# Filler matmuls in the setup, and PE transposes cut into thirds, in an attention and gated-MLP kernel

## The chip, the cores and the metric

The kernel runs on one core of one Trainium2 chip. A core has a matrix engine (TensorE, PE in the profile, with its weight loads as PEld), a vector engine (VectorE, DVE), an activation engine (ScalarE, ACT), GpSimd (POOL) and a queue engine (SyncE, SP), which here issues most transfers. All of them run beside each other and are held together by semaphores. The metric is the device time of one execution in microseconds; lower is better.

## What is computed

Block-sparse attention is followed by a gated MLP with a spatial projection, for 4 batches, 8 heads, 768 positions, head size 64:

```python
scores = scale * np.matmul(q, k.transpose(0, 1, 3, 2))
scores = np.where(mask, scores, -1000000000.0)       # window, global and sampled 32x32 blocks
attn = np.exp(scores - max);  attn = attn / attn.sum(-1)
x = np.matmul(attn, v)                               # heads joined: (4, 768, 512)
h = np.maximum(x @ w_in, 0.0)                        # 1024 wide
u, v = h[..., :512], h[..., 512:]
v_n = (v - mean(v)) / np.sqrt(var(v) + 1e-06)
v_s = np.einsum('ts,bsd->btd', w_spatial, v_n) + b_spatial[None, :, None]
out = (u * v_s) @ w_out
```

## The kernel before

Heads are taken in 16 pairs (p = 0 to 15, four pairs to a batch). A pair is 12 **slots** (s = 0 to 11), two heads of six key chunks. The main loop, lines 414 to 470, is an order written out by hand: it is the order in which every engine gets its instructions, and each engine works through its own in that order.

One slot does the following. `qk_exp` (L239) makes the scores of one chunk of 128 keys against all 768 queries, two PE matmuls of 384 columns into one of two PSUM buffers, and one ACT exponential (L248) that reads that buffer. The block mask is no separate step: 24 extra rows of `kt` (block indicator, `ind`) and `qt` (mask values, made once by the matmuls at L208) add a large negative number where a block is not allowed. `av` (L253) multiplies finished exponentials of seven slots ago with v, six PE matmuls of 65 columns; after each sixth, `norm` (L267) divides on DVE. A unit of the MLP of the batch before follows when there is one: `moe_units` (L313) makes them in four kinds (L332, L355, L377, L395), and they start in slot 9 of pair 4. In slot 8, `xtr` (L277) transposes the normalised output of the pair before, for three pairs of a batch by a DMA transpose on SP's queue and for the fourth by six PE transposes (L283) with a DVE copy behind them.

q and k come in as float32 and go through several hands. `load` (L91) puts three transfers of a pair on SP's queue, three pairs ahead, into two staging buffers per tensor. `prepare` (L116) casts them to bf16 on POOL, in slot 7, two pairs ahead. Then they have to be transposed. Pair 0 is done head by head on PE (`tr_head`, L188). Pairs 1 to 4 are done by `tr_pair` (L195): six PE transposes of 128x128 and two DVE copies, k and q each in one slot (slots 7 and 10 for pair 1, slots 5 and 9 after that). From pair 5 on, `tr_dma` (L225) issues DMA transposes on SP's queue in slot 10 two pairs ahead, and `split_pair` (L230) copies the halves to their places on DVE, k in slot 5 and q in slot 9. SP issues everything in program order, and an instruction that waits holds up those behind it; the same is true of DVE, where `split_pair(5, "k")` (slot 5 of pair 4) stands ahead of the last normalisation of pair 3 (slot 6).

The spatial weights (`ws_nat`) come in on POOL's queue, are transposed on PE in six units of six transposes (`wspt_unit`, L292) in slots 3, 7 and 11 of pairs 2 and 3, and are copied by DVE into `w_spt`. `w_in` and `w_out` follow on POOL's queue.

The setup (L122 to L221) starts the loads, runs eight PE matmuls on zeros into a scratch bank (L143 to L145), makes the mask's parts on POOL and DVE (`ind` is copied by POOL at L160 and moved into `kt` by DVE at L180), and transposes the first head.

Of the kernel before, what the change touches and what calls it, by code (L numbers as in the profile page):

```python
# [10 lines left out]
FP32 = mybir.dt.float32  # L11
BF16 = mybir.dt.bfloat16
I32 = mybir.dt.int32
AF = mybir.ActivationFunctionType
# [12 lines left out]
def kernel(  # L27
# [16 lines left out]
    nc = tc.nc  # L44

    B, H, S, D = q.shape
# [3 lines left out]
    NCH = S // 128  # L50
# [6 lines left out]
    NG = H // 2  # L57
    NP = B * NG
    MASK_NEG = -300.0
    VA = D + 1  # L60
    KR = D + NB
# [3 lines left out]
    psum = ctx.enter_context(tc.tile_pool(name="psum", bufs=1, space=bass.MemoryType.PSUM))  # L65
    ctx.enter_context(tc.manual_schedule())

    ident = const.tile([128, 128], BF16)
    warm = const.tile([128, 512], BF16)
    w_in_t = const.tile([128, NDM, DFF], BF16)  # L70
    w_out_t = const.tile([128, NDH, DM], BF16)
    ws_nat = const.tile([128, NCH, S], BF16)
# [4 lines left out]
    qt = [const.tile([KR, S], BF16, name=f"qt{s}") for s in range(4)]  # L77
    kt = [const.tile([KR, S], BF16, name=f"kt{s}") for s in range(4)]
# [18 lines left out]
    nat = {}  # L97
# [5 lines left out]
    def cast_qk(p, nm, hs, eng):  # L103
        src = st[nm, p][:, hs].rearrange("p h (c d) -> p h c d", d=D)
        dst = nat[nm, p].rearrange("p c h d -> p h c d")[:, hs]
        if eng is nc.scalar:
            nc.scalar.activation(out=dst, in_=src, func=AF.Copy)
        else:
            eng.tensor_copy(out=dst, in_=src)  # L109

    def cast_v(p):
        nc.gpsimd.tensor_copy(  # L112
            out=vv[p % 3][:, :, :, 0:D],
            in_=st.pop(("v", p)).rearrange("p h (c d) -> p h c d", d=D))
# [18 lines left out]
    ind_nat = const.tile([NB, S], BF16)  # L133
    ind = const.tile([NB, S], BF16)
# [5 lines left out]
    nc.vector.memset(tiny, 0.0)  # L140
    nc.scalar.activation(out=tiny, in_=tiny, func=AF.Exp)

    wps = psum.tile([128, 512], FP32, tag="moe", bufs=2)  # L143
    for _ in range(8):
        nc.tensor.matmul(out=wps, lhsT=warm[:, 0:128], rhs=warm, start=True, stop=True)  # L145


    colidx = const.tile([NB, NB], FP32)
# [8 lines left out]
    nc.gpsimd.affine_select(out=ind_nat, in_=ind_nat, compare_op=ALU.not_equal, fill=1.0,  # L157
                            base=0, pattern=[[-1, NB], [0, BLK]], channel_multiplier=1)
    make_identity(nc, ident)
    nc.gpsimd.tensor_copy(out=ind, in_=ind_nat.rearrange("b (p c) -> b c p", c=NCH))  # L160

    for s in range(3):
        nc.gpsimd.memset(vv[s][:, :, :, D:VA], 1.0)
# [13 lines left out]
                            op0=ALU.subtract, op1=ALU.mult)  # L177
    cast_qk(0, "q", slice(0, 1), nc.vector)
    cast_qk(0, "k", slice(0, 1), nc.scalar)
    nc.vector.tensor_copy(out=kt[0][D:KR, :], in_=ind)  # L180

    def dve_copy(o, i):
        nc.vector.tensor_copy(out=o, in_=i)

# [3 lines left out]
    def tr_head(h, nm, copy):  # L188
        ps = psum.tile([128, S], BF16, tag="moe", bufs=2)
        for c in range(NCH):  # L190
            nc.tensor.transpose(out=ps[0:D, c * 128:(c + 1) * 128], in_=nat[nm, 0][:, c, h],
                                identity=ident)
        copy((qt if nm == "q" else kt)[h][0:D, :], ps[0:D, :])

    def tr_pair(p, nm):  # L195
        src = nat.pop((nm, p))
        ps = psum.tile([128, S], BF16, tag="moe", bufs=2)
        for c in range(NCH):
            nc.tensor.transpose(out=ps[:, c * 128:(c + 1) * 128],
                                in_=src[:, c].rearrange("p h d -> p (h d)"), identity=ident)  # L200
        for h in range(2):
            nc.vector.tensor_copy(out=(qt if nm == "q" else kt)[(2 * p + h) % 4][0:D, :],
                                  in_=ps[h * D:(h + 1) * D, :])

    tr_head(0, "k", dve_copy)
    mq = psum.tile([128, 1024], FP32, tag="sc", bufs=2, name="mq")
    for hf in range(2):
        nc.tensor.matmul(out=mq[0:NB, hf * 512:hf * 512 + HALF], lhsT=bm,  # L208
                         rhs=ind[:, hf * HALF:(hf + 1) * HALF], start=True, stop=True)
    act_copy(qt[0][D:KR, :].rearrange("p (b c) -> p b c", b=2),  # L210
             mq[0:NB].rearrange("p (b c) -> p b c", b=2)[:, :, 0:HALF])
    tr_head(0, "q", dve_copy)

    def mask_rows(sl):
        nc.vector.tensor_copy(out=kt[sl][D:KR, :], in_=kt[0][D:KR, :])
        nc.vector.tensor_copy(out=qt[sl][D:KR, :], in_=qt[0][D:KR, :])

    def second_head():
        mask_rows(1)
        cast_qk(0, "k", slice(1, 2), nc.vector)  # L220
        cast_qk(0, "q", slice(1, 2), nc.vector)  # L221
# [3 lines left out]
    def tr_dma(p, nm):  # L225
        tt[nm, p] = work.tile([128, NCH, 128], BF16, tag=f"tt_{nm}", bufs=2, name=f"tt_{nm}")
        nc.sync.dma_start_transpose(out=tt[nm, p],
                                    in_=nat.pop((nm, p)).rearrange("p c h d -> p (c h d)"))

    def split_pair(p, nm):  # L230
        src = tt.pop((nm, p)).rearrange("x c n -> x (c n)")
        for h in range(2):
            nc.vector.tensor_copy(out=(qt if nm == "q" else kt)[(2 * p + h) % 4][0:D, :],
                                  in_=src[h * D:(h + 1) * D, :])
# [4 lines left out]
    def qk_exp(j, ci):  # L239
        if ci == 0:  # L240
            a_ref[j] = work.tile([128, NCH, S], BF16, tag="a_all", bufs=3, name="a_all")
        ps = psum.tile([128, 1024], FP32, tag="sc", bufs=2)
        for hf in range(2):
            nc.tensor.matmul(out=ps[:, hf * 512:hf * 512 + HALF],  # L244
                             lhsT=kt[j % 4][:, ci * 128:(ci + 1) * 128],
                             rhs=qt[j % 4][:, hf * HALF:(hf + 1) * HALF],
                             start=True, stop=True)
        nc.scalar.activation(  # L248
            out=a_ref[j][:, ci, :].rearrange("p (b c) -> p b c", b=2),
            in_=ps.rearrange("p (b c) -> p b c", b=2)[:, :, 0:HALF],  # L250
            func=AF.Exp, scale=0.125)
# [37 lines left out]
                in_=xn.rearrange("p c h d -> p (c h d)"))  # L289


    def wspt_unit(sc):  # L292
        def run():
            ps = psum.tile([128, S], BF16, tag="moe", bufs=2)
            for tcc in range(NCH):
                nc.tensor.transpose(
                    out=ps[:, tcc * 128:(tcc + 1) * 128],
                    in_=ws_nat[:, tcc, :].rearrange("p (s c) -> p c s", c=NCH)[:, sc, :],
                    identity=ident)
            nc.vector.tensor_copy(out=w_spt[:, sc, :], in_=ps)  # L300
        return run

    tail_tags = deque(["sc", "av", "moe"])

# [109 lines left out]
    for p in range(NP + 1):  # L414
        for s in range(12):
            g = 12 * p + s
            j, ci = divmod(g, NCH)
            if p == NP and g - LAG >= 2 * NP * NCH:
                break
            if p < NP:  # L420
                qk_exp(j, ci)
            if p == 0 and s == 0:
                second_head()
            if p == 0 and s == 3:
                tr_head(1, "k", dve_copy)
            if p == 0 and s == 4:
                tr_head(1, "q", dve_copy)
                mask_rows(2)
                mask_rows(3)
            if p + 1 < NP and s in ((5, 9) if p else (7, 10)):  # L430
                (split_pair if p + 1 > NG else tr_pair)(p + 1, "k" if s < 9 else "q")
            if s == 10 and NG < p + 2 < NP:
                tr_dma(p + 2, "k")
                tr_dma(p + 2, "q")
            if p == 0 and s == 0:
                cast_v(0)
                prepare(1)
                load(2)
                nc.gpsimd.dma_start(out=ws_nat,
                                    in_=moe_w_spatial.rearrange("(p c) s -> p c s", c=NCH))  # L440
            if s == 7 and p + 2 < NP:
                if p + 3 < NP:
                    load(p + 3)
                prepare(p + 2)
                if p == 0:
                    nc.gpsimd.dma_start(out=w_in_t,
                                        in_=moe_w_in.rearrange("(g p) f -> p g f", p=128))
                if p == 1:
                    nc.gpsimd.dma_start(out=w_out_t,
                                        in_=moe_w_out.rearrange("(g p) f -> p g f", p=128))  # L450
            if moe_q and slots_left > 0:
                budget += sum(u[0] for u in moe_q) / slots_left
                slots_left -= 1
                while moe_q and budget >= moe_q[0][0] / 2:
                    ns, run = moe_q.popleft()
                    run()
                    budget -= ns
            if g >= LAG:
                ja, qc = divmod(g - LAG, NCH)
                av(ja, qc)  # L460
                if qc == NCH - 1:
                    norm(ja)
            if p in (2, 3) and s % 4 == 3:
                wspt_unit((p - 2) * 3 + s // 4)()
            if s == 8 and p >= 1:
                xtr(p - 1)
                if p % NG == 0:
                    moe_q.extend(moe_units(p // NG - 1))
                    slots_left = 48
                    budget = 0.0  # L470
# [35 lines left out]
```

## Time and profile before

| | |
|---|---|
| median of 5 runs | 231.08 us (230.32 to 231.60) |
| the profiled execution | 231.09 us, of which its span is 229.31 |
| mean granted TensorE clock | 0.978 |
| PE busy | 218.2 us (95%) |
| ACT busy | 171.3 us (75%) |
| DVE busy | 132.8 us (58%) |
| POOL busy | 52.7 us (23%) |

Two rows of the page show the span in 40 slices of 5.7 us, each digit a share in tenths. They are ACT's busy share and the granted clock:

```profile
ACT  3669999996799767796799666987798677257341
PEclk9659999999999999999999999999999999999999
```

Slices 2 and 3 show a lower clock and ACT at six tenths; then ACT is full from slice 4 to slice 9, and after that only for a slice or two at a time. In the page's list of the costliest groups the exponential takes 810 ns, the score matmul 334 ns and the attention matmul 195 ns each; these are lengths from start to end, and matmuls overlap their neighbours, so for sums the distance from one start to the next is used.

### The profile page before, as it was taken

The page shows a single profiled execution, that of the slowest core. Times are in us where ns is not written, and L with a number is a line of the kernel's source. Part 1 is how long each engine was busy: PE and PEld are TensorE (multiplying, and loading weights), DVE is VectorE, ACT ScalarE, POOL GpSimd, SP SyncE. Part 2 cuts the span into 40 slices and gives each one's busy share as a digit, 9 for nine tenths or more (in the row PEclk, how much of TensorE's full clock was granted, in tenths as well). Part 3 has the DMA queues.
Part 4 walks back from the last instruction along what each step waited for, and adds up shares of the span by engine and source line. Part 5 has one row for each costly group of instructions (what it writes and reads, how often), then busy time and mean ns, then how long its engine had stood idle before and what let it go on. Part 6 is the DMA issues. An engine that isn't in the chain of part 4 may idle for free.

```text
span 229.3 us, 5275 instructions
## 1 busy us (share of the span) xinstructions
PE 218.2 (95%) x2134; PEld 130.4 (57%) x2134; DVE 132.8 (58%) x285; ACT 171.3 (75%) x244; POOL 52.7 (23%) x83
## 2 busy tenths in 40 slices
PE   7799999998999999999999999999999999999993
PEld 2356677765565555666656555566665555544541
DVE  6643555638996535339995444269992423575532
ACT  3669999996799767796799666987798677257341
POOL 7540650430144401210172301210260000012000
PEclk9659999999999999999999999999999999999999
DMA  6689999999518373989838263999050423520015
GB/s 204 208 237 226 362 178 247 229 230 289 182 34 202 98 137 61 272 277 281 262 69 243 59 117 67 276 321 266 3 103 3 80 48 76 195 88 0 0 47 229
DMA packets 54940, 37.31 MB, mean 163 GB/s; under 512 B 38404, under 2 KB 51204, under 8 KB 54788
## 3 DMA queue, kind: packets, MB, share of 16 engines
q1 hardware_dynamic: 53428, 33.83, 55.5%
q0 software_dynamic: 1200, 2.75, 6.9%
q10 hardware_dynamic: 288, 0.39, 0.5%
q8 instruction: 16, 0.26, 0.4%
q14 instruction: 8, 0.07, 0.1%
HBM read 24.38 MB, written 6.29 MB: 134 GB/s over the span
## 4 chain that ended last, share of the span: by engine, by line
PE 78%; ACT 12%; DMA 4%; DVE 3%; issue 1%; POOL 0%; ACTq 0%
PE ps L244 23%; ACT a_all L248 12%; PE ps_av L260 11%; PE ps_moe L377 10%; PE ps_moe L332 7%; PE ps_moe L395 7%; PE ps_moe L355 7%; DMA tt_k<-nat_k 3%; PE ps_t L377 2%; PE ps_t L332 2%; PE ps_t L355 2%; PE ps_t L395 2%; PE ps_sc L377 1%; DMA samp_i<-in_sampled_blocks_dram 1%; PE ps_sc L395 1%
## 5 line engine op out<-in xcount | busy, mean ns | idle before, releaser
L248 ACT ACTIVATE a_all<-ps 128x768 bf16<-128x768 f32 x192 | 144.2, 810 | 33.2 <-PE ps L244 32.6
L244 PE MATMUL ps<-qt,kt 88*128 88x384 bf16 x384 | 96.4, 334 | 5.0 <-ACT a_all L248 3.7
L260 PEld LDWEIGHTS <-a_all 128*128 128x128 bf16 x1152 | 61.9, 98 | 31.7 <-issue 0.7
L260 PE MATMUL ps_av<-vv,a_all 128*128 128x65 bf16 x1152 | 68.4, 195 | 0.0
L244 PEld LDWEIGHTS <-kt 88*128 88x128 bf16 x384 | 28.4, 99 | 11.0 <-issue 7.3
L380 DVE SCALAR_TENSOR_TENSOR gn<-ps_moe,b_col,un 128x512 bf16<-128x512 f32 x18 | 13.5, 751 | 27.4 <-PE ps_moe L377 27.4
L377 PE MATMUL ps_moe<-vn,w_spt 128*128 128x512 bf16 x108 | 26.3, 379 | 0.0
L112 POOL CAST vv<-st_v 128x768 bf16<-128x768 f32 x16 | 13.4, 839 | 52.8 <-PE ps_av L260 42.3
L377 PEld LDWEIGHTS <-w_spt 128*128 128x128 bf16 x144 | 13.8, 97 | 14.2
L345 POOL TENSOR_SCALAR std<-mv 128x3 f32<-128x3 f32 x8 | 1.9, 242 | 75.0 <-DVE mv L342 62.8
L109 POOL CAST nat_k<-st_k 128x768 bf16<-128x768 f32 x15 | 12.5, 834 | 26.8 <-DMA st_k<-in_k_dram 14.4
L274 DVE TENSOR_TENSOR xn<-ps_av,rc 128x384 bf16<-128x384 f32 x32 | 17.8, 558 | 1.4 <-DVE rc L273 0.3
L355 PE MATMUL ps_moe<-w_in_t,xt 128*128 128x512 bf16 x72 | 18.5, 379 | 0.0
L332 PE MATMUL ps_moe<-w_in_t,xt 128*128 128x512 bf16 x72 | 18.5, 378 | 0.0
L395 PE MATMUL ps_moe<-w_out_t,gt 128*128 128x512 bf16 x72 | 18.5, 379 | 0.0
L341 DVE BATCH_NORM_STATS2 stats<-vsb 128x6 f32<-128x512 bf16 x24 | 16.7, 695 | 1.9 <-ACT vsb L336 1.3
L332 PEld LDWEIGHTS <-xt 128*128 128x128 bf16 x96 | 9.3, 97 | 10.0 <-DVE xt L285 0.6
L402 DVE COPY osb<-ps_moe 128x512 f32<-128x512 f32 x9 | 6.2, 692 | 15.0 <-PE ps_moe L395 14.9
L355 PEld LDWEIGHTS <-xt 128*128 128x128 bf16 x96 | 9.3, 97 | 9.6
L395 PEld LDWEIGHTS <-gt 128*128 128x128 bf16 x96 | 8.9, 97 | 8.4
L359 DVE TENSOR_SCALAR vn<-vsb,mv,rstd 128x512 bf16<-128x512 bf16 x24 | 12.7, 564 | 0.6 <-POOL rstd L347 0.5
L273 DVE RECIPROCAL rc<-ps_av 128x6 f32<-128x6 f32 x32 | 6.0, 187 | 12.1 <-PE ps_av L260 12.0
(85 smaller groups left out, 181.7 us busy)
## 6 DMA issues: line engine op xcount, KB each, us to landing
st_v<-in_v_dram SPq DMA_DIRECT2D x16, 384.0 KB, 5.8
out_dram<-osb SPq DMA_DIRECT2D x24, 256.0 KB, 2.2
st_q<-in_q_dram SPq DMA_DIRECT2D x15, 384.0 KB, 4.5
st_k<-in_k_dram SPq DMA_DIRECT2D x15, 384.0 KB, 4.9
ws_nat<-in_moe_w_spatial_dram POOLq DMA_DIRECT2D x1, 1152.0 KB, 12.7
w_in_t<-in_moe_w_in_dram POOLq DMA_DIRECT2D x1, 1024.0 KB, 11.2
w_out_t<-in_moe_w_out_dram POOLq DMA_DIRECT2D x1, 512.0 KB, 11.5
st_k<-in_k_dram ACTq DMA_DIRECT2D x2, 192.0 KB, 2.9
```

Of the source, the lines that this page charges most:

```text
L112: nc.gpsimd.tensor_copy(out=vv[p % 3][:, :, :, 0:D], in_=st.pop(("v", p)).rearrange("p h (c d) -> p h c d", d=D))
L244: nc.tensor.matmul(out=ps[:, hf * 512:hf * 512 + HALF], lhsT=kt[j % 4][:, ci * 128:(ci + 1) * 128], rhs=qt[j % 4][:, hf * HALF:(hf + 1) * ...
L248: nc.scalar.activation(out=a_ref[j][:, ci, :].rearrange("p (b c) -> p b c", b=2), in_=ps.rearrange("p (b c) -> p b c", b=2)[:, :, 0:HALF], ...
L260: nc.tensor.matmul(out=av_ref[j][:, qc, :], lhsT=a_ref[j][:, ci, qc * 128:(qc + 1) * 128], rhs=vv[p % 3][:, h, ci, :], start=(ci == 0), st ...
L274: nc.vector.tensor_tensor(out=xn_ref[p][:, :, h, :], in0=ps[:, :, 0:D], in1=rc.to_broadcast([128, NCH, D]), op=ALU.mult)
L332: nc.tensor.matmul(out=ps, lhsT=xt(g)[:, tcc * 128:(tcc + 1) * 128], rhs=w_in_t[:, g, DH:DFF], start=(g == 0), stop=(g == NDM - 1))
L341: nc.vector.bn_stats(out=stats, in_=vsb[:, tcc, :])
L355: nc.tensor.matmul(out=ps, lhsT=xt(g)[:, tcc * 128:(tcc + 1) * 128], rhs=w_in_t[:, g, 0:DH], start=(g == 0), stop=(g == NDM - 1))
L359: nc.vector.tensor_scalar(out=vn[:, tcc, :], in0=vsb[:, tcc, :], scalar1=mv[:, tcc, 0:1], scalar2=rstd[:, tcc:tcc + 1], op0=ALU.subtract, ...
L377: nc.tensor.matmul(out=ps, lhsT=w_spt[:, sc, tcc * 128:(tcc + 1) * 128], rhs=vn[:, sc, :], start=(sc == 0), stop=(sc == NCH - 1))
L380: nc.vector.scalar_tensor_tensor(out=gn[:, tcc, :], in0=ps, scalar=b_col[:, tcc:tcc + 1], in1=un[:, tcc, :], op0=ALU.add, op1=ALU.mult)
L395: nc.tensor.matmul(out=ps, lhsT=gt[:, tcc, dhc, :], rhs=w_out_t[:, dhc, :], start=(dhc == 0), stop=(dhc == NDH - 1))
```

## The change

1. Setup. The scratch bank of the warm-up matmuls moves from the `moe` buffers to the `av` buffers, and the loop becomes a function `keep_warm(n, cols)`. Besides the eight matmuls of 512 columns it is called for two of 128 columns behind the first k transposes, for six behind the first q transposes, and for two in each of the slots 0 to 5 of pair 0. These matmuls multiply zeros and nothing reads their result.
2. `ind` is copied by ACT instead of POOL, and DVE moves it into `kt` behind the copy of the transposed k instead of ahead of it.
3. `tr_pair` does its six transposes in three steps of two, in three slots in a row: for pair 1 k in slots 6 to 8 and q in 9 to 11, for pairs 2 to 4 k in 4 to 6 and q in 7 to 9. The DVE copies come with the last step.
4. The transposes of the spatial weights are cut in the same way: nine thirds in each of pairs 2 and 3, one or two per slot, in slots 0 to 3, 10 and 11.

Everything from pair 4 on is unchanged in the program, with the DMA transposes and their copies.

```diff
-    wps = psum.tile([128, 512], FP32, tag="moe", bufs=2)
-    for _ in range(8):
-        nc.tensor.matmul(out=wps, lhsT=warm[:, 0:128], rhs=warm, start=True, stop=True)
+    wps = psum.tile([128, 512], FP32, tag="av", bufs=2)
+
+    def keep_warm(n, cols):
+        for _ in range(n):
+            nc.tensor.matmul(out=wps[:, 0:cols], lhsT=warm[:, 0:128], rhs=warm[:, 0:cols],
+                             start=True, stop=True)
+
+    keep_warm(8, 512)
...
-    nc.gpsimd.tensor_copy(out=ind, in_=ind_nat.rearrange("b (p c) -> b c p", c=NCH))
...
-    nc.vector.tensor_copy(out=kt[0][D:KR, :], in_=ind)
-
+    nc.scalar.activation(out=ind, in_=ind_nat.rearrange("b (p c) -> b c p", c=NCH),
+                         func=AF.Copy)
...
-    def tr_pair(p, nm):
-        src = nat.pop((nm, p))
-        ps = psum.tile([128, S], BF16, tag="moe", bufs=2)
-        for c in range(NCH):
+    tr_ps = {}
+
+    def tr_pair(p, nm, third):
+        if third == 0:
+            tr_ps[nm] = psum.tile([128, S], BF16, tag="moe", bufs=2, name="ps_tr")
+        src, ps = nat[nm, p], tr_ps[nm]
+        for c in (2 * third, 2 * third + 1):
             nc.tensor.transpose(out=ps[:, c * 128:(c + 1) * 128],
                                 in_=src[:, c].rearrange("p h d -> p (h d)"), identity=ident)
-        for h in range(2):
-            nc.vector.tensor_copy(out=(qt if nm == "q" else kt)[(2 * p + h) % 4][0:D, :],
-                                  in_=ps[h * D:(h + 1) * D, :])
+        if third == 2:
+            nat.pop((nm, p))
+            for h in range(2):
+                nc.vector.tensor_copy(out=(qt if nm == "q" else kt)[(2 * p + h) % 4][0:D, :],
+                                      in_=ps[h * D:(h + 1) * D, :])
 
     tr_head(0, "k", dve_copy)
+    nc.vector.tensor_copy(out=kt[0][D:KR, :], in_=ind)
+    keep_warm(2, 128)
...
     tr_head(0, "q", dve_copy)
+    keep_warm(6, 128)
...
-    def wspt_unit(sc):
-        def run():
-            ps = psum.tile([128, S], BF16, tag="moe", bufs=2)
-            for tcc in range(NCH):
...
+    ws_ps = {}
+
+    def wspt_third(i):
+        sc, third = divmod(i, 3)
+        if third == 0:
+            ws_ps[0] = psum.tile([128, S], BF16, tag="moe", bufs=2, name="ps_ws")
+        ps = ws_ps[0]
+        for tcc in (2 * third, 2 * third + 1):
+            nc.tensor.transpose(
...
+        if third == 2:
             nc.vector.tensor_copy(out=w_spt[:, sc, :], in_=ps)
-        return run
...
+            if p == 0 and s < 6:
+                keep_warm(2, 128)
...
-            if p + 1 < NP and s in ((5, 9) if p else (7, 10)):
-                (split_pair if p + 1 > NG else tr_pair)(p + 1, "k" if s < 9 else "q")
+            if p + 1 <= NG:
+                first = 4 if p else 6
+                if first <= s < first + 3:
+                    tr_pair(p + 1, "k", s - first)
+                elif first + 3 <= s < first + 6:
+                    tr_pair(p + 1, "q", s - first - 3)
+            elif p + 1 < NP and s in (5, 9):
+                split_pair(p + 1, "k" if s == 5 else "q")
...
-            if p in (2, 3) and s % 4 == 3:
-                wspt_unit((p - 2) * 3 + s // 4)()
+            if p in (2, 3) and not 4 <= s < 10:
+                for i in range(3 * (s if s < 4 else s - 6) // 2, 3 * (s + 1 if s < 4 else s - 5) // 2):
+                    wspt_third(9 * (p - 2) + i)
```

## The prediction

> **What bounds the kernel now.** The view of stretches first: busy time of each engine in 5 us pieces, the granted TensorE clock in the third column from the right.
>
> ```profile
> 10.00:15.00 5.00, 4.81 (x25) 2.39 (x26) 2.25 (x6) 3.38 (x6) 2.44 (x4) 0.50 0.55 189
> 15.00:20.00 5.00, 4.95 (x56) 3.52 (x54) 2.23 (x5) 3.84 (x6) 1.59 (x2) 0.69 1.02 199
> 20.00:25.00 5.00, 4.81 (x62) 3.40 (x62) 1.98 (x5) 4.91 (x8) 0.43 (x1) 1.00 0.98 301
> 50.00:55.00 5.00, 4.11 (x50) 2.62 (x47) 3.36 (x8) 3.80 (x6) 0.83 (x1) 1.00 0.93 241
> 55.00:60.00 5.00, 5.00 (x53) 3.07 (x52) 4.53 (x10) 3.86 (x6) 0.00 (x0) 1.00 1.15 315
> ```
>
> Three regimes. To 18 us PE runs at half clock and ACT starves (3.38 of 5). From 20 to 50 ACT is full (4.91 to 4.98 of 5). From 53 on PE is full, to the end. In half-us stretches the clock falls at 7.91 (0.91 means 0.09 of the half us lost, so 0.09 us before 8.00) and returns at 18.15:
>
> ```profile
> 7.50:8.00 0.50, 0.39 (x3) 0.10 (x1) 0.50 (x1) 0.40 (x1) 0.50 (x1) 0.91 1.05 393
> 18.00:18.50 0.50, 0.50 (x9) 0.43 (x8) 0.00 (x0) 0.34 (x2) 0.00 (x0) 0.85 0.94 194
> ```
>
> What joins the last two regimes is in the chain that ended last (start, length, what):
>
> ```profile
> 44.69 6.24 DMA tt_k<-nat_k
> 50.93 0.02 issue
> 50.96 1.02 DVE kt L233
> 51.98 0.01 issue
> 51.99 0.35 DVE kt L233
> ...
> 52.48 0.57 DVE xn L274
> 53.05 0.05 issue
> 53.10 0.51 PE ps L283 x6
> ```
>
> So the PE stage begins when a DMA transpose lands, not when ACT is ready. The timelines of POOL, the SP queue and DVE say what the transpose itself waits for:
>
> ```profile
> 41.87 0.83 POOL L109 CAST nat_k<-st_k 128x768 bf16<-128x768 f32 x1 [7.80 <-DMA st_k<-in_k_dram]
> 44.69 1.68 SPq L227 DMA_TRANSPOSE tt_k<-nat_k  x1
> 50.96 1.39 DVE L233 COPY kt<-tt_k 64x768 bf16<-64x768 bf16 x2 [3.24 <-DMA tt_k<-nat_k]
> ```
>
> POOL idled 7.80 us for pair 5's k. Asked by issue, that load left at 28.63 and took 13.1 us; pair 6's v left at 40.22 and took 7.9 (landing 48.1); the transpose of xn behind it took 5.5 (48.9), then tt_k landed at 50.93. One queue, nearly full since 12 us (DMA share 0.98 to 1.36 from 15 to 50): this chain is paced by transfers.
>
> **The change, part by part.**
>
> Setup. `ind` moves from POOL (1.19 us) to ACT; nearest rows: DVE's copy of the same shape 0.35, ACT's 24x768 from PSUM 0.80. I take 0.8. It starts after ACT's cast (done 3.72) and ends near 4.5, and its reader mq waits for `bm` until 5.37: free. DVE's `kt<-ind` (0.35) goes behind `kt<-ps` (0.55); both still end before the q transposes let DVE go on at 6.47. Eight 128-column fillers cost 8 x 0.054 = 0.43 us (six 512-column matmuls take 1.30, so 2.37 columns per ns) and lie in PE's waits before mq and, 0.75 us, before the first score matmul. First scores stay at 7.07, first exponential at 7.60. If that cover failed, at most 0.4 late.
>
> Fillers in slots 0 to 5: 12 x 0.054 = 0.65 us. With the clock full a slot needs 2 x 0.16 (scores) + 0.11 (fillers), plus 0.32 in slots 3 and 4 for a head's six transposes: 0.43 to 0.75, against ACT's 0.745 per exponential (26 take 19.25). Hidden. At half clock they would cost 1.3 us.
>
> Do they hold the clock? By column counts, in 4.49 to 7.91, the stretch before the drop, PE streamed 12 transposes, two mq and four score matmuls: 0.96 us without transposes, 1.60 with, of 3.41: 28% and 47%. The leanest stretch that kept the clock, 18.15 to 21.6, has 61% and 71%. The Trainium skill (TensorE: Matmul & The Clock Gate, Part 4) holds that transposes do not count as activity in the same way. By that rule the fillers lift the stretch to about 46% and the later slots to 57%, below anything the trace shows held; with transposes counted it is 65% and 70 to 75%, nearly the held row. I take the row: held. If the rule is right, one stretch at half clock is lost, four slots at 2 x 0.32 + 0.21 = 0.85 instead of 0.745 or some 0.5 us, and the fillers, which then fill PE, bring the clock back after it (85% without transposes did so at 18.15, 56% did not).
>
> Gain of the start: before, ten exponentials took 7.60 to 18.31 = 10.7 us; back to back 7.45. Minus 3.3. Given back: pair 1's q thirds now end in slot 11, so its copy (0.57) makes the first scores of pair 1 some 0.3 late. Net lead 2.9 us; with one stretch at half clock about 2.4.
>
> Thirds. Same number of transposes and copies; a slot with six takes PE 0.87 instead of 0.55, one with two 0.66. Under ACT's 0.745 that hardly showed: ACT's gaps from 20 to 50 sum to 0.33 us, so 0 to 0.3. Two covers get thin: the first spatial third needs ws_nat, landing at 11.63 + 12.7 = 24.3, at slot 24, now about 25.1; pair 3's k cast ends 27.4, needed at 28.4. Both hold by 0.8 and 1.0. Program order on SP and POOL is unchanged; only the waits of the xn transposes (34.46 and 43.39) release 3 us sooner.
>
> **What is late next.** With a lead of 2.9, slot 56 (the one before PE's transposes of xn at L283) starts its scores at 48.8 instead of 51.64 and its work ends near 49.6. But DVE stands in `split_pair(5, "k")`, queued ahead of pair 3's last normalisation, until tt_k lands. That landing follows the loads: casts of POOL wait for st_k and st_v, SP for casts, and from 12 us to the cast at 41.87 one cast alone was released by compute, a v cast at 33.23 that no transfer then waited for. Earliest possible: issue at 42.70 (cast done) and the same 6.24, landing 48.9; latest: behind pair 6's loads as before, 50.9. xn's earlier transpose only queues behind the same loads, so I take 50.9. One thing improves: kt's first copy took 1.02 against 0.35 for the second because POOL cast v from 50.94; that cast waits for attention of pair 3 and for its load (48.1), and now runs near 48.8. So copies end at 51.65, xn at 52.45, PE goes on at 52.5 instead of 53.1: **minus 0.6**. The other 2.3 us of lead are waited away.
>
> And PE is now idle from 49.6 to 52.5, 2.9 us instead of 0.78. The same page (Part 1) asks for an idle window of some 3.4 us before the clock drops, and warns only of gaps over about 3 us: by the rule, 2.9 costs nothing and the sum stays at -0.6. The row speaks against it: at 7.91 the clock fell though PE's longest gap in the stretch was 0.75, with 28 to 47% streamed. With 2.9 us idle wherever the window edges lie, one window streams at most about 45%. By the row the clock drops, into the PE-bound stage: one 3.41 us stretch at half speed is 1.7 us less PE work, about 1.6 at PE's 95%; if the edge falls inside the gap, the next window is only 60% busy, the clock is not returned, and it is 2.9. I take the row, 1.7.
>
> Sum: -0.6 + 1.7 = +1.1. The profiled execution was 231.09 (span 229.31 + 1.78), equal to the median 231.08. **Forecast 232.2.**
>
> **Cases.** (1) Chance 0.55: lead swallowed by tt_k, clock drops. 231.8 (1.35 lost) to 233.4 (2.9 lost).
> (2) 0.20: swallowed, clock stays (the page's rule, or a lead of under 1 us because the fillers do not hold the clock at the start for longer than the stretch costed above, so that the change does not do what it says). 231.1 - 0.6 = 230.5, spread 230.1 to 231.0. For it: the page, and that nothing in this trace shows a pure gap of 2.9. Against: the drop at 7.91.
> (3) 0.25: the transpose lands earlier because it is issued earlier. With landing 48.9 PE goes on at 50.5: -2.6, **228.5**; free of the wait altogether, 49.7: 227.7. For it: 6.24 us from issue to landing is double the 3.5 median of its group, and the transfers stand nearly still at times near 43 and 50. Against: the v load ahead of it landed only at 48.1.
>
> A measurement of this kernel can tell about 0.3% (0.7 us) from none. Faster: case 3 and a third of case 2, 0.32. Same: most of case 2, a little of 1, 0.15. Slower: 0.53. The likeliest case's own range is 231.8 to 233.4; the stated one reaches down to 228.3 for case 3 and leaves out its lower part and case 1's top.
>
> **What would show it.** Granted clock 1.00 from 8 to 18 and ACT near 4.9 of 5 there: the start. DVE idle about 6 us before kt<-tt_k, landing 50.5 to 51: swallowed. PE idle near 2.9 before L283's successor: the gap. A stretch of 0.50 between 50 and 57: case 1. I am wrong if tt_k lands before 50, or if the clock stays 1.00 after the gap.

## The result, and the profile after

The changed kernel takes **233.16 us** (median of 43 runs, 229.35 to 237.81); the kernel before, in 80 runs on the same chips, 231.58 (229.93 to 236.96). The ratio is 1.0023 with a 95% interval of 1.0003 to 1.0042. That ratio leaves out every run more than 1.5% above its kernel's best, here 27 of the changed kernel's 44 and among them all 14 in which the loss described below came more than once; by the medians of all runs the change costs 0.7%. The forecast was 232.2; its likeliest case ran from 231.8 to 233.4.

The profiled execution took 233.17 us, its span 231.4, 2.1 more than before. Its view of stretches (busy time and count of PE, PEld, DVE, ACT, POOL, then granted clock, DMA share, GB/s):

```profile
5.00:10.00 5.00, 5.00 (x31) 2.88 (x29) 2.70 (x7) 1.85 (x3) 1.58 (x2) 1.00 0.83 277
10.00:15.00 5.00, 4.83 (x44) 3.08 (x43) 2.26 (x6) 4.75 (x7) 2.36 (x4) 1.00 0.60 196
15.00:20.00 5.00, 4.37 (x64) 3.29 (x62) 2.97 (x6) 4.58 (x8) 1.59 (x2) 1.00 1.05 228
50.00:55.00 5.00, 1.91 (x20) 1.21 (x18) 2.29 (x7) 1.71 (x3) 0.00 (x0) 0.98 1.08 257
55.00:60.00 5.00, 5.00 (x40) 2.80 (x39) 3.02 (x6) 2.46 (x4) 0.00 (x0) 0.68 1.14 316
```

The start does what the change says: from 10 to 20 ACT now works 4.75 and 4.58 of 5 us, where it had 3.38 and 3.84. But from 50 to 55 PE works 1.91 instead of 4.11, and from 55 to 60 it is full at a clock of 0.68. (The 1.00 from 5 to 10 is not to be trusted. The clock's record starts with its first change, which here is the rise at 10.40; before it the page shows 1.00, although the warm-up matmuls are 427 ns apart, twice their distance at full clock. So a clock row is only good behind its first change.) In stretches of half a microsecond the clock falls at 54.78 and returns at 58.19, one piece of 3.41 us:

```profile
54.50:55.00 0.50, 0.50 (x4) 0.24 (x2) 0.47 (x3) 0.50 (x1) 0.00 (x0) 0.78 1.03 363
58.00:58.50 0.50, 0.50 (x3) 0.25 (x2) 0.00 (x0) 0.27 (x1) 0.00 (x0) 0.81 1.02 356
```

The chain that ended last (start, length, what) still goes through the same DMA transpose:

```profile
43.81 8.20 DMA tt_k<-nat_k
52.01 0.02 issue
52.03 0.35 DVE kt L245
52.38 0.01 issue
52.39 0.35 DVE kt L245
...
52.89 0.57 DVE xn L286
53.45 0.05 issue
53.50 0.51 PE ps L295 x6
```

And the timelines of POOL, DVE and PE (start, length; in brackets the idle time before it and what ended that) show who waited. PE's line of the kernel before comes first:

```profile
53.10 0.51 PE L283 MATMUL ps<-ident,xn 128*128 128x128 bf16 x6 [0.78 <-DVE xn L274]
```

```profile
42.72 0.83 POOL L109 CAST nat_k<-st_k 128x768 bf16<-128x768 f32 x1 [9.54 <-DMA st_k<-in_k_dram]
52.03 0.72 DVE L245 COPY kt<-tt_k 64x768 bf16<-64x768 bf16 x2 [6.52 <-DMA tt_k<-nat_k]
53.50 0.51 PE L295 MATMUL ps<-ident,xn 128*128 128x128 bf16 x6 [3.09 <-DVE xn L286]
```

Every wait on this way has grown: POOL's for the load from 7.80 to 9.54, DVE's for the transpose from 3.24 to 6.52, PE's from 0.78 to 3.09. Compute came sooner and the transfer did not, so PE goes on at 53.50 (before: 53.10), after an idle gap that takes its clock.

One number orders all that follows. **From the first matmul of the MLP to the end of the span a kernel needs about 175.4 us with the clock full** (before: 53.94 to 229.3; of the kernels below, 175.4 with the gap filled and with the thirds only, 175.7 with pair 5 on PE, and 175.9 to 176.5 in three in which PE waits once more behind that point); PE is the bound there. So the time is the moment at which the MLP can go on, plus what is lost behind it. After: 54.34 + 175.4 = 229.7, and 1.7 more for one stretch at half clock makes 231.4.

How often the stretch is lost can be read from every execution's mean clock, since one stretch is half of 3.41 us of 231, or 0.0074:

| mean clock of the changed kernel | executions | median us |
|---|---|---|
| 1.00, none | 2 | 230.1 |
| 0.991 to 0.993, one stretch | 28 | 232.73 |
| 0.984 to 0.985, two | 13 | 234.03 |
| 0.978, three | 1 | 237.81 |

(A start at half clock before the first change is in no record, so this counts losses behind it.)

### The profile page after: what moved, and what is told of

Its sections match the earlier page's. It is cut to its first block, busy times and chain, and to the rows that moved or that the text cites. A ratio compares the mean times of both kernels' runs of the same rounds, so it can differ in the third digit from the quotient of the medians.

```text
span 231.4 us, 5315 instructions
## 1 busy us (share of the span) xinstructions
PE 219.5 (95%) x2154; PEld 132.7 (57%) x2154; DVE 130.8 (57%) x285; ACT 171.5 (74%) x245; POOL 51.2 (22%) x82
## 4 chain that ended last, share of the span: by engine, by line
PE 88%; ACT 5%; DMA 4%; DVE 2%; issue 1%
PE ps L256 27%; PE ps_av L272 13%; PE ps_moe L393 10%; PE ps_moe L348 7%; PE ps_moe L411 7%; PE ps_moe L371 7%; ACT a_all L260 5%; DMA tt_k<-nat_k 4%; PE wps L147 2%; PE ps_t L393 2%; PE ps_t L348 2%; PE ps_t L371 1%; PE ps_t L411 1%; PE ps_tr L206 1%; PE ps_sc L393 1%; PE ps L195 1%
## 5 line engine op out<-in xcount | busy, mean ns | idle before, releaser
L256 PE MATMUL ps<-qt,kt 88*128 88x384 bf16 x384 | 95.4, 330 | 3.7 <-ACT a_all L260 2.8
L272 PEld LDWEIGHTS <-a_all 128*128 128x128 bf16 x1152 | 61.0, 98 | 29.7 <-issue 0.6
L256 PEld LDWEIGHTS <-kt 88*128 88x128 bf16 x384 | 28.9, 98 | 7.3 <-issue 4.5
L348 PE MATMUL ps_moe<-w_in_t,xt 128*128 128x512 bf16 x72 | 19.3, 391 | 0.0
L371 PE MATMUL ps_moe<-w_in_t,xt 128*128 128x512 bf16 x72 | 18.5, 378 | 0.0
L354 DVE TENSOR_SCALAR vsb<-ps_moe 128x512 bf16<-128x512 f32 x18 | 12.3, 682 | 2.4 <-PE ps_moe L348 2.4
```

The source lines that it names most:

```text
L256: nc.tensor.matmul(out=ps[:, hf * 512:hf * 512 + HALF], lhsT=kt[j % 4][:, ci * 128:(ci + 1) * 128], rhs=qt[j % 4][:, hf * HALF:(hf + 1) * ...
L272: nc.tensor.matmul(out=av_ref[j][:, qc, :], lhsT=a_ref[j][:, ci, qc * 128:(qc + 1) * 128], rhs=vv[p % 3][:, h, ci, :], start=(ci == 0), st ...
L348: nc.tensor.matmul(out=ps, lhsT=xt(g)[:, tcc * 128:(tcc + 1) * 128], rhs=w_in_t[:, g, DH:DFF], start=(g == 0), stop=(g == NDM - 1))
L371: nc.tensor.matmul(out=ps, lhsT=xt(g)[:, tcc * 128:(tcc + 1) * 128], rhs=w_in_t[:, g, 0:DH], start=(g == 0), stop=(g == NDM - 1))
```

## The experiments

Ratios are against the kernel before, run in the same series; line numbers are each kernel's own.

**Fill the gap.** Twelve matmuls of 512 columns on zeros go in front of the PE transposes of xn, where PE waits. If the idle PE loses the clock, this gives it back; the lead stays swallowed.

```diff
             if s == 8 and p >= 1:
+                if p == NG:
+                    gap = psum.tile([128, 512], FP32, tag="moe", bufs=2, name="gap")
+                    for _ in range(12):
+                        nc.tensor.matmul(out=gap, lhsT=warm[:, 0:128], rhs=warm,
+                                         start=True, stop=True)
                 xtr(p - 1)
```

> Twelve filler matmuls of 512 columns (12 x 0.216 = 2.6 us at full clock) stand in PE's order just ahead of the transposes that wait for xn. Theory A (lead waited away at tt_k, and the idle gap costs the clock): PE goes on at the same moment, near 53.5, tt_k lands near 52 as before, but the granted clock stays 1.00 after the gap; 1.6 us (one stretch at half clock) to 2.9 (two) come off: about 230.8. Theory B (the slower stretch behind the gap costs little, since ACT and DVE are the limit there): no change against the changed kernel, 232.5. If the fillers are longer than the gap, PE goes on later than 53.5 and the run is slower by that much.

Measured: 230.88 us (22 runs), ratio 0.9992 (0.9973 to 1.0011). In 19 of the 22 the mean clock is 0.996 or more. Its stretches, where the first two numbers behind the comma are PE's:

```profile
50.00:55.00 5.00, 4.28 (x37) 2.23 (x35) 3.08 (x8) 0.92 (x3) 1.33 (x2) 1.00 1.09 308
55.00:60.00 5.00, 4.95 (x51) 2.90 (x50) 4.52 (x10) 4.21 (x6) 0.00 (x0) 1.00 1.09 311
```

PE is busy with nothing useful, the clock stays at 1.00, and 2.3 us of the median come back (1.8 if each median is set against the kernel before of its own series, 231.58 and 231.14). The MLP starts at 53.55, no sooner than before (53.94), and the kernel is no faster than before. So the two parts are apart: the swallowed lead makes the gain zero, the clock turns it into a loss.

**Take the copies out of the way.** The two `split_pair` of pair 5 move from slots 5 and 9 to slots 10 and 11 of pair 4, behind the last normalisation of pair 3. Nothing then stands in front of it on DVE.

```diff
-            elif p + 1 < NP and s in (5, 9):
-                split_pair(p + 1, "k" if s == 5 else "q")
+            elif p + 1 < NP and s in ((10, 11) if p == NG else (5, 9)):
+                split_pair(p + 1, "k" if s in (5, 10) else "q")
```

> The changed kernel with the copies of pair 5's transposed k and q moved from slots 5 and 9 of pair 4 to slots 10 and 11, behind the last normalisation of pair 3 on DVE. Theory A (DVE standing in that copy is the only thing that holds PE at pair 4): xn is made about 2.5 us sooner, PE's gap of 3 us goes, the clock stays 1.00, and the whole lead of the start reaches the end: about 228.0. Theory B (something else, such as the transposed x of the earlier pairs or the k of pair 5 itself, is late by the same amount): PE stops a few slots later, 230.5 or more.

Measured: **228.82 us** (227.67 to 229.77, 7 runs, all with the clock kept), ratio 0.9907 (0.9874 to 0.9940). The lead arrives: slot 8's transposes run at 48.67 instead of 53.50. The 228.0 of theory A is missed by 0.8, for its chain shows what is late next:

```profile
40.58 10.20 DMA xt<-xn
50.77 0.05 issue
50.82 0.62 PE ps_moe L348 x2
```

The MLP's first matmul runs at 49.33, then PE stands for the DMA transpose of pair 2's output, which took 10.20 us, and a little later for pair 5's copies:

```profile
50.82 0.61 PE L348 MATMUL ps_moe<-w_in_t,xt 128*128 128x512 bf16 x2 [1.11 <-DMA xt<-xn]
54.16 0.50 PE L256 MATMUL ps<-qt,kt 88*128 88x384 bf16 x2 [0.64 <-DVE qt L245]
```

The MLP goes on at 50.82, about 3 us sooner than before, and the span is 2.6 less (226.7).

**The same move without the change.** The kernel before, with pair 5's copies in slots 10 and 11. It tells whether the move alone is worth something.

```diff
-            if p + 1 < NP and s in ((5, 9) if p else (7, 10)):
-                (split_pair if p + 1 > NG else tr_pair)(p + 1, "k" if s < 9 else "q")
+            if p + 1 <= NG and s in ((5, 9) if p else (7, 10)):
+                tr_pair(p + 1, "k" if s < 9 else "q")
+            elif NG < p + 1 < NP and s in ((10, 11) if p == NG else (5, 9)):
+                split_pair(p + 1, "k" if s in (5, 10) else "q")
```

> The kernel before with only the move of pair 5's copies to slots 10 and 11 of pair 4. Theory A (before, DVE's wait for tt_k held PE by 0.8 us only, because compute itself was late): 0.5 to 0.9 us off, about 230.5. Theory B (the wait is worth its full 3 us of DVE idle): 228.5.

Measured: 231.4 us (14 runs), ratio 1.0031 (1.0010 to 1.0052). All the expectations missed: it is no gain at all. Its DVE timeline says why:

```profile
55.29 0.69 DVE L338 TENSOR_SCALAR vsb<-ps_moe 128x512 bf16<-128x512 f32 x1 [0.64 <-PE ps_moe L332]
56.01 0.69 DVE L341 BATCH_NORM_STATS2 stats<-vsb 128x6 f32<-128x512 bf16 x1
56.74 0.18 DVE L342 BATCH_NORM_AGGREGATE mv<-stats 128x2 f32<-128x6 f32 x1
56.84 0.70 DVE L233 COPY kt<-tt_k 64x768 bf16<-64x768 bf16 x2
```

The copies now queue behind the first MLP unit's work on DVE, and the scores of pair 5 wait for them until 57.99. Without the lead there is little on the other side to gain: in this execution, whose clock rose only at 20.07, ACT is the chain until 53.00 and the MLP starts at 54.38. Neither the warm start (1.0023) nor the late copies (1.0031) gains alone; together they do (0.9907).

**One half of the change each.** First only the thirds (no small fillers, `ind` back on POOL, the scratch bank back in `moe`); then only the setup (transposes uncut, in the slots they had before).

```diff
-    keep_warm(2, 128)
...
-    keep_warm(6, 128)
...
-            if p == 0 and s < 6:
-                keep_warm(2, 128)
```

> The thirds alone, setup and slots without fillers. Theory A: the clock stays at half until about 18 us, hardly any lead, PE's gap near 53 about 0.8 us as in the kernel before: 231.5, no change. Theory B (the thirds make a part of the lead): gap longer by that part, time 231 to 232.

```diff
-                first = 4 if p else 6
-                if first <= s < first + 3:
-                    tr_pair(p + 1, "k", s - first)
-                elif first + 3 <= s < first + 6:
-                    tr_pair(p + 1, "q", s - first - 3)
+                if s in ((5, 9) if p else (7, 10)):
+                    for t in range(3):
+                        tr_pair(p + 1, "k" if s < 9 else "q", t)
...
-            if p in (2, 3) and not 4 <= s < 10:
-                for i in range(3 * (s if s < 4 else s - 6) // 2, 3 * (s + 1 if s < 4 else s - 5) // 2):
+            if p in (2, 3) and s % 4 == 3:
+                for i in range(3 * (s // 4), 3 * (s // 4) + 3):
```

> Setup with fillers and the moved ind, but the transposes of q, k and the spatial weights in one piece in their old slots. Theory A (the fillers make the lead, the thirds hardly matter): as the changed kernel, clock full from about 10 us, PE gap of about 3 us near 50, clock lost behind it: 232.5. Theory B (the thirds matter for the lead): ACT loses 1 us or more between 8 and 20 us and the gap is shorter by that.

Measured, thirds only: 230.76 us (22 runs), ratio 0.9984 (0.9963 to 1.0005), no difference; the clock is half from 8.41 to 18.65 as before, and PE's gap at 52.72 is 0.79. Setup only: 232.82 us (9 runs), ratio 0.9959 (0.9900 to 1.0018), an interval too wide to tell it from the full change by time; by the medians of all its runs it is 0.7% slower than the kernel before, as the full change is. Seven of the nine lost clock (one stretch 232.82, two 234.4; kept, 229.02). Its trace tells more. The PE timeline:

```profile
54.13 0.82 PE L295 MATMUL ps<-ident,xn 128*128 128x128 bf16 x6 [4.39 <-DVE xn L286]
```

The gap is there, and longer. So the setup makes both the lead and the loss; cutting the transposes is worth nothing measurable, on either side. Which part of the setup does it (the fillers, `ind` on ACT or the other bank) these two runs leave open; the next two narrow it down for the fillers.

**Which fillers hold the clock.** First the twelve in slots 0 to 5 go and the eight of the setup stay; then all twenty small ones become PE transposes of the same size.

```diff
-            if p == 0 and s < 6:
-                keep_warm(2, 128)
```

> The changed kernel without the twelve fillers in slots 0 to 5; the eight in the setup stay. In the first stretch PE streams about 1.4 us of 3.41 without transposes (41%), 60% with them, later ones 47% and 66% or less. Theory A (a stretch under about 45% without transposes loses the clock): the clock drops once or more between 8 and 18 us, the lead shrinks, and so does PE's gap near 50; time like the kernel before, 231.5. Theory B (60% with transposes is enough): as the changed kernel, 232.5.

```diff
+    wpt = psum.tile([128, 1024], BF16, tag="av", bufs=2, name="wpt")
+
+    def keep_warm_tr(n):
+        for _ in range(n):
+            nc.tensor.transpose(out=wpt[:, 0:128], in_=warm[:, 0:128], identity=ident)
...
-    keep_warm(2, 128)
+    keep_warm_tr(2)
...
-    keep_warm(6, 128)
+    keep_warm_tr(6)
...
-                keep_warm(2, 128)
+                keep_warm_tr(2)
```

> The changed kernel with its twenty 128-column fillers made as PE transposes of the same size, so that PE streams the same columns. Theory A (transposes do not count as activity): the clock drops near 8 us as in the kernel before and stays at half to 15 or 18 us, little lead, 231.5. Theory B (they count): clock and time as the changed kernel, 232.5.

Measured: 232.9 us (6 runs), ratio 1.0095 (1.0059 to 1.0132), and 233.4 us (6 runs), 1.0102 (1.0058 to 1.0146). Both held the clock through the start and lost it at the handover, after gaps of 5.07 and 3.48 us. So the twelve slot fillers are not needed, and transposes count for the clock: the second kernel's stretch from 4.47 to 7.88 has 28.1% of its time in matmuls and 37.5% in transposes and was held, and the kernel before lost its clock at 28.1% and 18.8%. Theory B holds for both. No run takes the setup's eight fillers alone away.

**What stands behind the gain of the late copies.** Three more kernels start from the moved copies or replace them. In all three, pair 2's output is transposed on PE instead of by DMA:

```diff
-        if p % NG == NG - 1:
+        if p % NG == NG - 1 or p == NG - 2:
```

The first has the copies in slots 10 and 11 as above, the second in slots 9 and 10, and the third leaves them in slots 5 and 9 but makes pair 5's k and q transposes on PE too:

```diff
-            if p + 1 <= NG:
+            if p <= NG:
                 first = 4 if p else 6
...
-            if s == 10 and NG < p + 2 < NP:
+            if s == 10 and NG + 1 < p + 2 < NP:
                 tr_dma(p + 2, "k")
```

> The split-late kernel, with pair 2's output also transposed on PE (six transposes and a DVE copy in slot 8 of pair 3) instead of by a DMA behind the loads. In the split-late run PE stood until that DMA landed at 50.8. Theory A (that landing is now what starts the gated MLP): PE goes on near 49.3, 1 to 1.5 us off the split-late kernel's 228.8: 227.5. Theory B (the w_in transfer, or tt_k for pair 5's first scores, comes next at nearly the same moment): 228.5 or more.

> As the run with pair 2's output on PE, but pair 5's copies in slots 9 and 10 instead of 10 and 11, ahead of the first MLP unit's work on DVE. Theory A (the 0.64 us that pair 5's first scores waited for those copies is what late copies cost): 0.3 to 0.6 us off that run's 229.0: 228.5. Theory B (DVE then waits for tt_k again, and the MLP's first copies stand behind it): 229.0 or more.

> The changed kernel, with pair 5's k and q transposed on PE in thirds as pairs 1 to 4 (so that no DMA transpose stands in DVE's way at pair 4) and pair 2's output transposed on PE. Theory A (PE and ACT were held at pair 4 by those DMA transposes and by nothing else): neither the 3 us gap nor the 0.64 us wait of the split-late runs; the lead of the start less 0.6 us of PE work for twelve more transposes: 227.5 to 228.5, clock 1.00 after the start, and under 0.9 % below any split-late run. Theory B (DVE's gated-MLP work or ACT is then the limit, so that the lead can't be had): 229 or more.

Measured:

| kernel | us | ratio | MLP starts | span |
|---|---|---|---|---|
| slots 10 and 11 | 229.03 (19 runs) | 0.9930 (0.9907 to 0.9952) | 50.54 | 227.1 |
| slots 9 and 10 | 229.3 (6 runs) | 0.9885 (0.9830 to 0.9939) | 50.4 | 230.0 |
| pair 5 on PE | 229.6 (22 runs) | 0.9938 (0.9917 to 0.9958) | 51.84 | 227.6 |

Taking away the 10.20 us transfer gained nothing measurable (theory B's 228.5 or more, but not for its reason). At slots 10 and 11 the MLP starts at 50.54 instead of going on at 50.82, and at 54.15 PE stands 0.64 us for pair 5's q copy, as it did with the transfer in place. The new transposes have a cost of their own: in slot 8 of pair 3 they wait for a normalisation that stands on DVE behind the two copies of pair 4's k, and ACT then runs dry for 0.71 us, in all three kernels. In that of slots 10 and 11:

```profile
40.70 0.51 PE L295 MATMUL ps<-ident,xn 128*128 128x128 bf16 x6 [0.40 <-DVE xn L286]
41.58 2.21 ACT L260 ACTIVATE a_all<-ps 128x768 bf16<-128x768 f32 x3 [0.71 <-PE ps L256]
```

Slot 56 begins at 49.20, where it began at 48.15 with the transfer in place; the 0.71 is most of that. At slots 9 and 10 the k copy comes too early again and waits for its transfer, and the first MLP unit's work on DVE waits behind it, with the q copy behind that. The DVE timeline of that kernel:

```profile
52.00 1.25 DVE L245 COPY kt<-tt_k 64x768 bf16<-64x768 bf16 x2 [1.31 <-DMA tt_k<-nat_k]
```

In that execution PE stood 1.70 us at 55.09 and one stretch at half clock followed. Four of its six runs kept the clock (median 228.59), two did not (231.8 and 232.7), so it is not settled whether it beats the late copies. With pair 5 on PE, DVE has the copies in front of the normalisation all the same:

```profile
48.68 1.12 DVE L211 COPY kt<-ps_tr 64x768 bf16<-64x768 bf16 x2 [3.71 <-PE ps_tr L206]
49.84 0.20 DVE L285 RECIPROCAL rc<-ps_av 128x6 f32<-128x6 f32 x1
50.07 0.56 DVE L286 TENSOR_TENSOR xn<-ps_av,rc 128x384 bf16<-128x384 f32 x1
```

No transfer is waited for any more, and the MLP starts 1.0 later than it goes on with the late copies; 229.6 is theory B's "229 or more". The best version that always kept its clock is the change with the copies in slots 10 and 11: 0.9% faster than the kernel before; its interval overlaps those of the other two at 0.993 and 0.9938.

## Why the prediction was right, point by point

The first case, "lead swallowed by tt_k, clock drops", is what happened, and the sign and size of the median (233.16 against 232.2) follow from it. By its steps:

- **What bounds the kernel.** Right: the chain of the changed kernel goes through the same transpose, and the move of two copies, which touches only who waits for it, changed the result by 1.9% (233.16 to 228.82; 1.7% if each is set against the kernel before of its own series).
- **The setup is free.** Right in cost, though `ind` on ACT took 1.21 us and not 0.8. "First exponential 7.60" missed: 8.90 in the profiled execution, 7.19 to 8.05 in eight kernels with this setup or a variant of it. The eight large matmuls ran from 1.18 to 4.78 there and lay across two stretches of 3.41 us, with 75% and 84% of each streamed at half clock (counted as in the last section); the clock rose only after the third, at 10.40. Where those stretches lie differs from one execution to the next.
- **The fillers hold the clock.** Right, by the row and not by the rule: "with transposes counted" was the choice that the run with transposes as fillers confirms. Its leanest held stretch was misread: with transposes counted, 48.86 to 52.28 of the kernel before has 66% and no transposes, less than the 71% named, and 65% lies right at it.
- **"Net lead 2.9".** Slot 56 began its scores at 49.73 where 48.8 was forecast (before: 51.64): a lead of 1.9 in this execution, whose clock came late. Where it came by 6.1, slot 56 began between 47.63 (no slot fillers) and 49.06 (setup only), leaving out the kernels with pair 2 on PE: leads of 2.6 to 4.0, so 2.9 was a fair figure for those.
- **The thirds.** Right: ACT stood 0.42 us behind pair 1's last q third (forecast 0.3), and the thirds alone measure 0.9984 with 1 inside the interval.
- **"So I take 50.9."** This term of the sum was mis-sized. The transpose landed at 52.0. Though the load in front of it came 0.85 later than before (cast at 42.72 against 41.87), it was issued 0.88 sooner (43.81 against 44.69); but from issue to landing it took 8.20 instead of 6.24. PE went on at 53.50, not 52.5, so "minus 0.6" became +0.4. In the kernels with a lead and the copies in slot 5 (gap filled, setup only, no slot fillers, transposes as fillers, and the change itself) it landed between 50.75 and 52.65; in the two without a lead at 50.93 and 50.67. That the lead brought it no sooner is shown; whether a lead makes it later, or one execution differs from another by as much, no run here settles.
- **The kt copies.** Right: 0.35 and 0.35, where the first had 1.02 beside POOL's cast.
- **PE idle 2.9, and the clock drops.** Right in kind: 3.09, and 42 of 44 executions lost at least one stretch. That the gap is so near to 2.9 is in part luck: PE's work ended at 50.41 and not at 49.6, and PE went on at 53.50 and not at 52.5, two misses of 0.8 and 1.0 that cancel. The page's rule would have kept the clock; the row decided. (The warning of gaps over some 3 us stands in the closing table of TensorE: Matmul & The Clock Gate, not in its Part 1.) The price of 1.7 was 1.66 in the profiled execution: 231.4 less 54.34 less 175.4. The possibility of 2.9 for two stretches measured 3.3 (234.03 against 230.7 for the runs of the filled gap that kept the clock), or 2.9 when the 0.44 between the two series' kernels before is taken off.

Sum of the profiled execution: +0.4 and +1.7 make 2.1, for +1.1 forecast; all of the difference is the landing of the transpose.

Of the rivals, the second (clock kept, 230.5) is what the filled gap built on purpose: 230.7. The third, an earlier transpose, did not come; what it priced as "free of the wait altogether", 227.7, measured 228.8 with the copies moved, where two further waits of PE (1.11 for pair 2's transpose, 0.64 for pair 5's copies) come up.

## What to carry to other kernels

A lead won in one stage is worth what the next wait leaves of it: follow it to the first instruction that waits for a transfer, and look at what is queued behind that instruction on its engine. Where that next stage is bound by the engine that now idles, the idling is not free: a few microseconds can cost the clock at the start of the bound stage, and filler work in the gap or a later place for the waiting instruction gives it back. Two edits can each be worth nothing and be worth a per cent together, so a rejected move is to be tried again when what hid it is gone.

## What the runs showed of the hardware

**The clock goes by the share streamed in fixed stretches of 3.41 us, and transposes count.** In each trace the changes of the clock lie a whole number of such stretches apart (after: 10.40, then 13 stretches to 54.78, then one to 58.19). Matmuls of 512 columns follow each other at 427 ns at half clock, so a stretch holds 4096 columns at half clock and 8192 at full. Counted from the traces, each matmul in the stretch in which it starts, as shares of 8192:

| kernel | matmuls | transposes | sum | clock after it |
|---|---|---|---|---|
| after, 51.36 to 54.78 | 28.1% | 9.4% | 37.5% | dropped |
| pair 2 on PE, slots 9 and 10, 52.67 to 56.08 | 40.8% | 0 | 40.8% | dropped |
| thirds only, 5.00 to 8.41 | 28.1% | 14.1% | 42.2% | dropped |
| after, 47.95 to 51.36 | 45.6% | 0 | 45.6% | held |
| before, 4.49 to 7.91 | 28.1% | 18.8% | 46.9% | dropped |
| no slot fillers, 7.43 to 10.85 | 37.5% | 18.8% | 56.2% | held |
| transposes as fillers, 4.47 to 7.88 | 28.1% | 37.5% | 65.6% | held |

In the twelve traces no stretch at full clock with a sum under 43% was held and none over 47% dropped. Between the two the count can't order them, since one score matmul at an edge of a stretch is 4.7%. Matmuls alone don't sort the rows: 28.1% stands on both sides, and 37.5% was held where 40.8% dropped. That a transpose counts in full is not shown: the last row needs no more than about a third of its transposes to pass the 40.8% that dropped. This stands against two sentences of the Trainium skill (TensorE: Matmul & The Clock Gate): Part 4, by which transposes do not count in the same way, if that is read as not at all, and Part 1, which asks for an idle window of some 3.4 us. Before, the clock dropped with no gap over 0.75 us, and in the second row with one of 1.70; after, with one of 3.09, of which 2.1 lay in the stretch that dropped. The way back needs more: no stretch at half clock with 81% or less of its 4096 columns brought it, from 84 to 94% some did and some did not, and every one from 97% on did.

**A mean clock of 1.00 can hide a cold start.** The kernel before with the late copies shows it: its page has 1.00 throughout, but the first entry of its clock's record is the rise at 20.07, and its score matmuls of 384 columns follow each other at 271 to 320 ns up to then and at some 162 ns after it. Of the kernel before, 12 of 47 executions of one series have a mean clock of 0.997 or more and a median of 231.82; the 35 with 0.978 or less have 230.78. A cold start of that kind would explain the difference, but no trace of those executions is kept.
